# Token blocks of 512 and 256 in place of 384, with high and low parts side by side in one product

## The chip, the cores and the metric

One core of one Trainium2 chip runs the whole program. The metric is the device time of one execution in microseconds, the median of the runs shown. Engines: TensorE (PE; its weight loads are PEld), VectorE (DVE), ScalarE (ACT), GpSimd (POOL) and SyncE (SP), which issues most DMAs.

## What is computed

Four batches of 768 tokens, 8 heads of 48. A decaying state per head gives the attention's rows, which become x with 384 columns a token; a low-rank mix over the tokens and a two-layer channel mix follow:

```
for t in range(S):
    cur = einsum('bhd,bhe->bhde', u[None] * kt, vt)
    y[:, :, t] = einsum('bhd,bhde->bhe', rt, state + cur)
    state = w[None, :, :, None] * state + einsum('bhd,bhe->bhde', kt, vt)
...
u  = x + (x^T @ U @ V)^T              # U: 768 x 32, V: 32 x 768
out = u + max(u @ w_ch1, 0) @ w_ch2   # 384 -> 1536 -> 384, float32
```

## The kernel before, in words

The attention works in chunks of 128 tokens, six a batch. For batches 1 to 3, `a_chunk` (L1081) does a chunk's products in one go into the accumulator banks "mm" and "av", with the next chunk's scores and state in "tr" and "sc"; VectorE masks, keeps the state and adds the results into x (L1111).

After six chunks `c_g` (L1180) sums U^T x on TensorE (L1172) and splits it into G (L1192 to L1197). For batch 0 and the first block of batch 1 (`inside`), u is turned in TensorE: `c_x` transposes x into banks and `c_xu` adds the low-rank product there. For all other blocks `c_u` (L1199) corrects x by one product and one VectorE addition (L1205), `c_store` writes it to DRAM, `c_blocks` (L1270) reads it back in 32 x 32 blocks, and `c_turn` (L1273) transposes 384 tokens at a time on VectorE (L1279), copies the result to the high part uTh on ScalarE (L1281) and subtracts for the low part uTl on VectorE or GpSimd (L1282).

The channel mix takes a batch in two blocks of 384 tokens (TB, TPB = 3 chunks). The hidden layer has 12 slices of 128. For each slice f, `m_1` (L1290) makes 9 products of 384 columns into one of two "mm" banks: for each of three column tiles high W1 x high u, low W1 x high u, high W1 x low u. ScalarE rectifies into hh (L1305), VectorE makes the low part hl (L1306). `m_2` (L1312) makes 9 more products, three for each chunk, into three "acc" banks that run over all 12 slices; then VectorE adds the bank to x (L1348) and SyncE stores the rows (in the last block, ScalarE's queue). Every product loads its weights first; all these products go through the helper `whole` (L382), so they show as L385, and the names tell them apart: p<-uTh,w1s is `m_1`, p<-w2s,hh is `m_2`.

Every operation is handed to `Plan` with a key (a planned time) and a cost. `Plan.schedule` issues on each engine, in an order fixed at build time, the ready operation of lowest key. A batch's `mlp_units` are `m_1` of slice f + 1, then `m_2` of slice f, 49 units of PER = 1.85 a batch; the attention chunks of the next batch lie between them, from 6 after the batch's begin in steps of 10.0 (batches 2 and 3), with `c_g` at their end:

```
begin = [T0 + 49 * PER * b for b in range(B)]
t0, per = ((begin[b - 1] + 30, 8.0), (begin[b - 1] + 6, 10.0))[b > 1]
end = attention(b, t0, per, 5.0, 0)
at(end, lambda b=b: c_g(b))
```

Of the kernel before, what the change touches and what calls it, by code (L numbers as in the profile page):

```python
# [47 lines left out]
class Plan:  # L48
# [107 lines left out]
    def schedule(self):  # L156
# [12 lines left out]
        def admit(o):  # L169
# [8 lines left out]
            for b in o.allocs:  # L178
                ring = self.rings[b.tag]
                i = min((i for i, f in enumerate(ring["free"]) if f is not None), key=lambda i: ring["free"][i][0])  # L180
                o.ends.append(ring["free"][i])
                if ring["last"] is not None:
# [138 lines left out]
def rwkv_moe(ctx: ExitStack, tc: tile.TileContext, r, k, v, w, u, U, V, w1, w2, out):  # L321
# [14 lines left out]
    TB = 384  # L336
    NTB = S // TB
    TPB = TB // 128
    NX = 11
    NXS = 4  # L340
    NH = 4
    NR = 2
# [143 lines left out]
    pwi = cbuf([PD, NP, C], F32, "pwi")  # L486
# [209 lines left out]
    def a_load(n):  # L696
        b, c = divmod(n, NCH)
        if n < 4:
            t3 = xbuf([128, 2 * H * HP + DM], F32, "uTl" if n % 2 else "uTh", 2, f"ld_{n}")
# [16 lines left out]
        for i, src in ((1, k), (0, r), (2, v)) if n < NQA else ((0, r), (1, k), (2, v)):  # L716
            eng = "ACT" if n < NQA and i == 1 else "SP"
            dma(lambda q, i=i, src=src: q.dma_start(part(i)[:, :, :D], src[b, :, c * C:(c + 1) * C, :].rearrange("h p d -> p h d")),  # L718
                [ts[i] if n < 4 else (t3, i)] if n < 4 else [(ts[i], "d")], after_weights(n), 1024, 192, eng=eng, late=1300 if (n, i) == (0, 0) else 0)
# [460 lines left out]
    def c_g(b):  # L1180
# [9 lines left out]
        gf = wbuf([R, DM], F32, "xl", NXS, f"gf_{b}")  # L1190
# [22 lines left out]
    def c_x(b, t, i):  # L1213
# [3 lines left out]
        x = xs[b * NCH + t * TPB + i]  # L1217
# [5 lines left out]
    def u_bufs(b, t):  # L1223
        uT[b, t] = (xbuf([128, NCT, TB], F32R, "uTh", 2, f"uTh_{b}_{t}"),
                    xbuf([128, NCT, TB], F32R, "uTl", 2, f"uTl_{b}_{t}"))

    def c_xu(b, t):
        u_bufs(b, t)
        uh, ul = uT[b, t]
        for ct in range(NCT):  # L1230
            pt = upt[b, t][ct]
            pe(200, lambda ct=ct, pt=pt: whole(pt.t[:, :TB], lhsT=Gs[b].t[:, ct * 128:(ct + 1) * 128],
                                               rhs=V3.t[:, t * TB:(t + 1) * TB],
                                               start=False, stop=True, skip_group_check=True), [pt], [Gs[b], V3])
            on_act(384, lambda ct=ct, pt=pt: nc.scalar.copy(uh.t[:, ct, :], pt.t[:, :TB]), [(uh, ct)], [pt])
            on_dve(384, lambda e, ct=ct, pt=pt: e.tensor_tensor(ul.t[:, ct, :], pt.t[:, :TB], f32(uh.t[:, ct, :]),  # L1236
                                                                ALU.subtract), [(ul, ct)], [pt, (uh, ct)])

    def c_ut(b, i):
        n = b * NCH + i  # L1240
        t, j = divmod(i, TPB)
        if j == 0:
            u_bufs(b, t)
        uh, ul = uT[b, t]
# [3 lines left out]
        ptv = pt.t[:, :DM].rearrange("p (c t) -> p c t", c=NCT)  # L1248
        sl = slice(j * 128, (j + 1) * 128)
        nc.scalar.copy(uh.t[:, :, sl], ptv)  # L1250
        nc.vector.tensor_tensor(ul.t[:, :, sl], ptv, f32(uh.t[:, :, sl]), ALU.subtract)
# [14 lines left out]

    def c_blocks(b, t, ct):

        bt = ublk[b, t, ct] = wbuf([128, TPB, 128], F32, "xh", NXS, f"ub_{b}_{t}_{ct}")
        dma(lambda q: q.dma_start(bt.t, ud[b].t[t * TPB:(t + 1) * TPB, 4 * ct:4 * ct + 4].rearrange("j k t e -> (k t) j e")),  # L1270
            [bt], [(ud[b], (i, j)) for i in range(t * TPB, (t + 1) * TPB) for j in range(2)], 384, 512, late=1000)

    def c_turn(b, t, ct):  # L1273
        if ct == 0:
            u_bufs(b, t)
        uh, ul = uT[b, t]
        bt = ublk.pop((b, t, ct))
        ut = wbuf([128, TB], F32, "xl", NXS, f"ut_{b}_{t}_{ct}")
        on_dve(680, lambda e: e.transpose(ut.t.rearrange("p (j t m) -> p j m t", t=32, m=4),  # L1279
                                          bt.t.rearrange("p j (m c) -> p j m c", c=32)), [ut], [bt])  # L1280
        on_act(384, lambda: nc.scalar.copy(uh.t[:, ct, :], ut.t), [(uh, ct)], [ut])  # L1281
        on_either(384, lambda e: e.tensor_tensor(ul.t[:, ct, :], ut.t, f32(uh.t[:, ct, :]), ALU.subtract), [(ul, ct)],  # L1282
                  [ut, (uh, ct)])
# [4 lines left out]
    MM = 174  # L1288

    def m_1(b, t, f):  # L1290
        uh, ul = uT[b, t]
        pt = bank("mm", f"p1_{b}_{t}_{f}")

        def part(ct):
            wt = W1[f].t
            fs = slice(ct * 128, (ct + 1) * 128)
            o = pt.t[:, :TB]
            whole(o, lhsT=wt[:, 0, fs], rhs=uh.t[:, ct, :], start=(ct == 0), stop=False)
            whole(o, lhsT=wt[:, 1, fs], rhs=uh.t[:, ct, :], start=False, stop=False)
            whole(o, lhsT=wt[:, 0, fs], rhs=ul.t[:, ct, :], start=False, stop=(ct == NCT - 1))  # L1300
        for ct in range(NCT):
            pe(3 * MM, lambda ct=ct: part(ct), [pt], [(uh, ct), (ul, ct), W1[f]])
        hh = xbuf([128, TB], F32R, "hh", NH, f"hh_{b}_{t}_{f}")
        hl = xbuf([128, TB], F32R, "hl", NH, f"hl_{b}_{t}_{f}")
        on_act(384, lambda: nc.scalar.activation(hh.t, pt.t[:, :TB], AF.Relu), [hh], [pt])  # L1305
        on_dve(384, lambda e: e.scalar_tensor_tensor(hl.t, pt.t[:, :TB], 0.0, f32(hh.t), ALU.max, ALU.subtract),  # L1306
               [hl], [pt, hh])
# [4 lines left out]
    def m_2(b, t, f, first, last):  # L1312

        hh, hl = hs.pop((b, t, f))
        for i in range(TPB):
            n = b * NCH + t * TPB + i
            if first:
                ops[n] = bank("acc", f"p2_{n}_{f}")

        def high(i, pt):  # L1320
            ts_ = slice(i * 128, (i + 1) * 128)
            for half in range(2):
                whole(pt.t[:, :DM], lhsT=hh.t[:, ts_], rhs=W2[f].t[:, half], start=(first and not gates and half == 0), stop=False)

        def low(i, pt):
            ts_ = slice(i * 128, (i + 1) * 128)
            whole(pt.t[:, :DM], lhsT=hl.t[:, ts_], rhs=W2[f].t[:, 0], start=False, stop=last > 0)
        def gate(i, pt):
            whole(pt.t[:, :DM], lhsT=V3.t[:, (t * TPB + i) * 128:(t * TPB + i + 1) * 128], rhs=Gs[b].t, start=True, stop=False)
        gates = f == 0 and inside(b, t)  # L1330
        if gates:
            for i in range(TPB):
                pt = ops[b * NCH + t * TPB + i]
                pe(MM, lambda i=i, pt=pt: gate(i, pt), [pt], [Gs[b], V3])
        parts = [(part, m, h, i) for part, m, h in ((high, 2, hh), (low, 1, hl)) for i in range(TPB)]
        late = [0] * TPB
        if b == B - 1 and t == NTB - 1:

            late = [PER * x for x in {NFT - 3: (0, 2.3, 4), NFT - 2: (0, 0.4, 2.1), NFT - 1: (0, 0.1, 1.2)}.get(f, late)]
        for part, m, h, i in sorted(parts, key=lambda p: late[p[3]]):  # L1340
            n = b * NCH + t * TPB + i
            pe(m * MM, lambda part=part, i=i, pt=ops[n]: part(i, pt), [ops[n]], [h, W2[f]], dk=late[i])
        if last:
            for i in range(TPB):
                n = b * NCH + t * TPB + i
                x, pt = xs[n], ops[n]
                s0 = (t * TPB + i) * 128
                on_dve(384, lambda e, x=x, pt=pt: e.tensor_tensor(x.t, pt.t[:, :DM], x.t, ALU.add), [x], [pt])  # L1348
                left[n] = left.get(n, NFT) - last
# [9 lines left out]
    def mlp_runs(b):  # L1359
# [3 lines left out]
        cuts = [0, NFT // 3, 2 * NFT // 3, NFT]  # L1363
        runs, done = [], [0, 0]
        for i, c in enumerate(cuts[1:] + [NFT]):
# [4 lines left out]
    def mlp_units(b):  # L1370
# [3 lines left out]
        units = []  # L1374
        for i in range(len(steps) + 1):
            if i < len(steps):
                units.append(lambda s=steps[i]: m_1(b, s[0], s[1]))
            if i:
                units.append(lambda s=steps[i - 1]: m_2(b, *s))
# [246 lines left out]
```

## Time and profile before

| what | us |
|---|---|
| median of three runs | 401.51 (401.1 to 402.57) |
| the profiled execution | 402.06 |
| its span, first to last instruction | 400.3 |
| TensorE busy | 391.6 |
| VectorE busy | 270.6 |
| ScalarE busy | 132.4 |
| GpSimd busy | 88.0 |

The products of the channel mix run from about 42 us to 396 us with the attention's between them; batch 1's first product is near 138.8 us, batch 2's at 230.4, batch 3's at 321.0. A product's duration is its latency, and products overlap: what one costs is the distance from its start to the next one's. Windows give the busy time of each engine in a stretch; a wait names who waited and what ended it.

### The profile page before, as it was taken

What the parts mean: (1) busy time and instruction counts of PE and PEld (TensorE: products, weight loads), DVE (VectorE), ACT (ScalarE), POOL (GpSimd) and SP (SyncE); (2) the same over time, 40 slices, a digit from 0 to 9 for tenths busy, and PEclk for the clock granted to TensorE, in tenths of its full rate; (3) what the DMA queues carried; (4) which work ended last, traced back from release to release, by engine and by line L of the source; (5) the groups of instructions that cost most, each with busy time, mean ns of one, the idle gap of its engine ahead of it and who ended that gap; (6) DMA issues with size and microseconds to landing.
All of it is one profiled execution on the core that took longest, in us unless ns stands there. A gap on an engine that the chain in (4) does not pass through costs nothing.

```text
span 400.3 us, 11670 instructions
## 1 busy us (share of the span) xinstructions
PE 391.6 (98%) x4833; PEld 377.6 (94%) x4833; DVE 270.6 (68%) x626; ACT 132.4 (33%) x344; POOL 88.0 (22%) x136
## 2 busy tenths in 40 slices
PE   7999999999999999999999999999999999999995
PEld 7797899999999999999999999999999999999995
DVE  5797999999999778897684588876423661222112
ACT  3547968467851312110132240120113221111110
POOL 2972142244422114131140131231000120000000
PEclk9999999999999999999999999999999999999999
DMA  9989998799778685873797777510103630001001
GB/s 141 169 158 291 171 230 195 117 213 230 124 110 180 101 197 83 149 121 61 147 167 111 147 169 120 95 33 2 61 2 61 123 117 0 2 0 62 1 2 63
DMA packets 189993, 45.27 MB, mean 113 GB/s; under 512 B 174701, under 2 KB 188398, under 8 KB 189934
## 3 DMA queue, kind: packets, MB, share of 16 engines
q1 hardware_dynamic: 186382, 43.28, 55.4%
q10 hardware_dynamic: 3552, 1.18, 1.3%
q8 instruction: 40, 0.66, 0.7%
q14 instruction: 19, 0.16, 0.1%
HBM read 36.77 MB, written 7.67 MB: 111 GB/s over the span
## 4 chain that ended last, share of the span: by engine, by line
PE 92%; DVE 3%; SPq 1%; DMA 1%; ACT 1%; issue 0%; POOL 0%; POOLq 0%; DVEq 0%
PE p L385 75%; PE pav L901 3%; PE pav L907 3%; DMA ub<-in_u_dram 1%; PE pav L1053 1%; PE bank_tr L881 1%; SPq L718 1%; PE bank_tr L867 1%; PE bank_tr L1004 1%; PE bank_tr L1172 1%; PE pav L1059 1%; DVE uTl L1236 1%; PE bank_sc L867 1%; PE bank_tr L818 1%; DVE raw_w L612 1%; PE ptr L818 0%
## 5 line engine op out<-in xcount | busy, mean ns | idle before, releaser
L385 PE MATMUL p<-uTh,w1s 128*128 128x384 f32 x576 | 148.6, 338 | 0.2 <-DVE w1s L647 0.2
L385 PE MATMUL p<-w2s,hh 128*128 128x384 f32 x576 | 119.3, 337 | 0.2 <-ACT hh L1305 0.2
L1305 ACT ACTIVATE hh<-p 128x384 fp32r<-128x384 f32 x96 | 47.2, 492 | 216.5 <-PE p L385 216.4
L1306 DVE SCALAR_TENSOR_TENSOR hl<-p,hh 128x384 fp32r<-128x384 f32 x96 | 53.3, 555 | 89.6 <-ACT hh L1305 88.7
L385 PEld LDWEIGHTS p<-uTh,w1s 128*128 128x128 f32 x576 | 102.9, 188 | 1.3 <-DVE w1s L647 0.5
L385 PEld LDWEIGHTS p<-w2s,hh 128*128 128x128 f32 x576 | 100.6, 188 | 1.3 <-ACT hh L1305 0.5
L385 PE MATMUL p<-uTl,w1s 128*128 128x384 f32 x288 | 96.6, 335 | 0.0
L385 PE MATMUL p<-w2s,hl 128*128 128x384 f32 x288 | 66.6, 334 | 0.0
L385 PEld LDWEIGHTS p<-uTl,w1s 128*128 128x128 f32 x288 | 54.0, 188 | 0.3 <-DVE uTl L1236 0.3
L385 PEld LDWEIGHTS p<-w2s,hl 128*128 128x128 f32 x288 | 51.5, 188 | 0.0
L1282 POOL TENSOR_TENSOR uTl<-ut,uTh 128x384 fp32r<-128x384 f32 x7 | 7.1, 1016 | 71.3 <-ACT uTh L1281 71.3
L901 PEld LDWEIGHTS pav<-vsw,am 64*64 64x64 f32 x288 | 17.4, 134 | 4.5 <-issue 4.2
L901 PE MATMUL pav<-vsw,am 64*64 64x48 f32 x288 | 19.8, 221 | 0.0
L768 POOL MEMSET ks<- 128x128 f32 x24 | 4.7, 205 | 67.6 <-PE bank_tr L881 67.5
L901 PE MATMUL pav<-ldv,am 64*64 64x48 f32 x288 | 19.3, 221 | 0.0
L907 PE MATMUL pav<-S,rT 48*64 48x48 f32 x528 | 19.1, 218 | 0.0
L778 POOL TENSOR_TENSOR dv<-ldr,ldk 128x384 f32<-128x384 f32 x14 | 14.3, 1020 | 20.6 <-DVE wm L529 8.8
L907 PEld LDWEIGHTS pav<-S,rT 48*64 48x64 f32 x528 | 17.3, 135 | 0.0
L901 PEld LDWEIGHTS pav<-ldv,am 64*64 64x64 f32 x288 | 17.0, 134 | 0.0
L1348 DVE TENSOR_TENSOR x<-p,x 128x384 f32<-128x384 f32 x30 | 15.0, 549 | 2.8 <-PE p L385 2.3
L789 ACT ACTIVATE dv<-ldv,dg 128x48 f32<-128x48 f32 x56 | 13.4, 321 | 2.8 <-DVE dg L785 2.7
L1111 DVE TENSOR_TENSOR x<-pav,dv 128x192 f32<-128x192 f32 x36 | 11.9, 348 | 2.8 <-PE pav L907 2.8
(192 smaller groups left out, 565.5 us busy)
## 6 DMA issues: line engine op xcount, KB each, us to landing
raw_w<-in_moe_w_ch_dram SPq DMA_DIRECT2D x24, 384.0 KB, 4.6
out_dram<-x SPq DMA_DIRECT2D x21, 192.0 KB, 3.0
ldr<-in_r_dram SPq DMA_DIRECT2D x20, 192.0 KB, 3.7
ldk<-in_k_dram SPq DMA_DIRECT2D x20, 192.0 KB, 4.4
ldv<-in_v_dram SPq DMA_DIRECT2D x20, 192.0 KB, 4.4
bl<-in_r_dram SPq DMA_DIRECT2D x79, 48.0 KB, 2.4
bl<-in_k_dram SPq DMA_DIRECT2D x79, 48.0 KB, 2.7
ub<-ud SPq DMA_DIRECT2D x15, 192.0 KB, 3.3
```

The lines of the kernel that those rows point to most:

```text
L385: return nc.tensor.matmul(*args, **kw)
L768: op("POOL", 250, lambda: nc.gpsimd.memset(ks.t[:, :, D:], 0.0), [(ks, "pad")], [])
L778: on_either(384, lambda e, a_=a_, b_=b_: e.tensor_mul(dv.t, a_()[:, :, :D], b_()[:, :, :D]), w_, r_, only="POOL" if front(n) else None)
L789: nc.scalar.activation(dv.t[:, h], vt()[:, h], AF.Copy, scale=dg.t[:, h:h + 1])
L867: return [lambda q=q, i=i: nc.tensor.matmul(pt.t[(i ^ j) * C2:(i ^ j) * C2 + C2, q * C2:(q + 1) * C2], lhsT=kT.t[rows, q, i * C2:(i + 1) * ...
L901: return nc.tensor.matmul(to(q, j, i), lhsT=am[j].t[half, q, :], rhs=vsw[n].t[half, q, :] if j else vt()[half, 2 * q, :], start=((alone or ...
L907: return nc.tensor.matmul(to(q, row, i), lhsT=rT.t[rows, q, i * C2:(i + 1) * C2], rhs=St[n, i].t[rows, q, :], start=False, stop=((alone or ...
L1111: return e.tensor_tensor(heads(x.t), heads(avp[n][bank_].t[:, :DM]), heads(of), ALU.add)
L1282: on_either(384, lambda e: e.tensor_tensor(ul.t[:, ct, :], ut.t, f32(uh.t[:, ct, :]), ALU.subtract), [(ul, ct)], [ut, (uh, ct)])
L1305: on_act(384, lambda: nc.scalar.activation(hh.t, pt.t[:, :TB], AF.Relu), [hh], [pt])
L1306: on_dve(384, lambda e: e.scalar_tensor_tensor(hl.t, pt.t[:, :TB], 0.0, f32(hh.t), ALU.max, ALU.subtract), [hl], [pt, hh])
L1348: on_dve(384, lambda e, x=x, pt=pt: e.tensor_tensor(x.t, pt.t[:, :DM], x.t, ALU.add), [x], [pt])
```

## The change

Batches 1 to 3 take blocks of 512 and 256 tokens (4 and 2 chunks); batch 0 keeps 384. In the block of 512 the products of `m_1` have 512 columns, and `m_2` has a fourth chunk whose sums lie in the bank "av" and are added to x before each attention chunk that needs the bank (`cuts`). In the block of 256 the high and the low u lie side by side in one buffer: per column tile one product low W1 x high u (256 columns) and one high W1 x both (512 columns, the whole bank); VectorE adds the bank's halves into a new buffer `hs`, from which the rectifier and the low part read; `m_2` there is two units later, not one. Transposes are of 256 tokens. u's buffers become one ring of four, hl has three buffers for four, two rings of small buffers three for four, x has twelve for eleven; `c_u` takes two banks, not three. The keys change: units of 2.5 and 1.15 for the two blocks (1.85 in batch 0), attention chunks 9.3 apart, `c_g` and what follows 4.0 sooner.

```
-    TB = 384
-    NTB = S // TB
-    TPB = TB // 128
-    NX = 11
-    NXS = 4
+    NTB = 2
+    HB = 256
+    def tb(b, t):
+        return (512, 256)[t] if b else S // NTB
+    def joined(b, t):
+        return b > 0 and t == 1
+    NX = 12
+    NXS = 3
     NH = 4
+    NHL = 3
...
-        pt = bank(("tr", "sc", "av")[i % 3], f"ph_{n}") if b < B else bank("mm", f"ph_{n}")
+        pt = bank(("tr", "sc")[i % 2], f"ph_{n}") if b < B else bank("mm", f"ph_{n}")
...
+    class Parts:
+        def __init__(self, b, t):
+            self.n, self.joined = tb(b, t), joined(b, t)
+            self.bufs = [xbuf([128, NCT, 512 if b else self.n], F32R, "uT", 4, f"uT{'hl'[i]}_{b}_{t}") for i in range(2 - self.joined)]
+        def at(self, i, ct, lo=0, hi=None):
+            c0 = i * self.n if self.joined else 0
+            return self.bufs[0 if self.joined else i].t[:, ct, c0 + lo:c0 + (self.n if hi is None else hi)]
+        def both(self, ct):
+            return self.bufs[0].t[:, ct, :]
...
+        ut = wbuf([128, HB], F32, "xl", NXS, f"ut_{b}_{t}_{ct}_{g}")
+        on_dve(400, lambda e: e.transpose(ut.t.rearrange("p (j t m) -> p j m t", t=32, m=4),
+                                          bt.t[:, 2 * g:2 * g + 2].rearrange("p j (m c) -> p j m c", c=32)), [ut], [bt])
...
+            if joined(b, t):
+                whole(o, lhsT=wt[:, 1, fs], rhs=u.at(0, ct), start=(ct == 0), stop=False, skip_group_check=True)
+                whole(pt.t, lhsT=wt[:, 0, fs], rhs=u.both(ct), start=False, stop=(ct == NCT - 1), skip_group_check=True)
+                return
...
+        if joined(b, t):
+            rd = wbuf([128, HB], F32, "hs", 1, f"hs_{b}_{f}")
+            src = lambda: rd.t
+            on_dve(2 * n, lambda e: e.tensor_reduce(src(), pt.t.rearrange("p (i n) -> p n i", i=2), AX.X, ALU.add), [rd], [pt], dk=SUM)
...
+            if starts(b, t, f, i, first):
+                ops[n] = bank("acc" if i < 3 else "av", f"p2_{n}_{f}")
...
+            due.append(i)
+            while due and (i + 1 == len(steps) or due[0] + 1 + joined(b, steps[due[0]][0]) <= i):
+                j = due.pop(0)
+                units.append((steps[j][0], 2, steps[j][1], lambda s=steps[j]: m_2(b, *s)))
...
+    def starts(b, t, f, i, first):
+        return first if t or i < 3 or not 0 < b < B else cuts[b, f][0]
+    def ends_(b, t, f, i, last):
+        return last if t or i < 3 or not 0 < b < B else cuts[b, f][1]
+    def chunk_times(b):
+        t0, per = ((begin[b - 1] + 30, 8.0), (begin[b - 1] + 6, 9.3))[b > 1]
+        return t0, per
...
+        keys = [x for c in range(NCH) for t0, per in [chunk_times(b + 1)] for x in [t0 + per * c]] if b + 1 < B else []
...
+            end = f in ends or any(x < k <= ms[j + 1][0] for k in keys)
+            cuts[b, f] = (first, n if end else 0)
...
-    T0, PER = 44.0, 1.85
+    T0, PERS, SOON = 44.0, (2.5, 1.15, 1.85), 4.0
...
-            end = attention(b, t0, per, 5.0, 0)
+            end = attention(b, t0, per, 5.0, 0) - (SOON if b > 1 else 0)
```

## Rows read from the trace of the kernel before

**Rows 1.** The page: its first line, parts 1 and 4 (by engine).

```profile
span 400.3 us, 11670 instructions
...
PE 391.6 (98%) x4833; PEld 377.6 (94%) x4833; DVE 270.6 (68%) x626; ACT 132.4 (33%) x344; POOL 88.0 (22%) x136
...
PE 92%; DVE 3%; SPq 1%; DMA 1%; ACT 1%; issue 0%; POOL 0%; POOLq 0%; DVEq 0%
```

**Rows 2.** The chain of waits, 300 to 400 us: start us, us, what.

```profile
310.26 85.84 PE p L385 x495
396.09 0.02 issue
396.12 0.56 DVE x L1348
```

**Rows 3.** Windows by stage: us, busy us by engine (instructions), granted clock, DMA share, GB/s.

```profile
138.00:188.00 50.00, 49.77 (x790) 47.93 (x789) 40.83 (x101) 7.93 (x16) 12.79 (x20) 1.00 0.71 124
188.00:209.00 21.00, 21.00 (x280) 20.39 (x279) 15.63 (x37) 4.25 (x13) 5.78 (x6) 1.00 0.79 142
209.00:230.00 21.00, 21.00 (x163) 20.61 (x162) 11.18 (x20) 6.13 (x15) 1.02 (x1) 1.00 0.77 132
...
301.00:321.00 20.00, 20.00 (x123) 19.90 (x115) 10.19 (x19) 5.74 (x14) 1.01 (x1) 1.00 0.54 104
```

**Rows 4.** The list of waits: us in total, times, longest.

```profile
ACT hh L1305 <- PE p L385: 216.4, 82, 5.9
DVE hl L1306 <- ACT hh L1305: 88.7, 53, 2.8
```

**Rows 5.** Groups by line and shape, TensorE: count, busy us, mean ns, idle before.

```profile
L385 PE MATMUL p<-uTh,w1s 128*128 128x384 f32 x576 | 148.6, 338 | 0.2 <-DVE w1s L647 0.2
...
L385 PEld LDWEIGHTS p<-uTh,w1s 128*128 128x128 f32 x576 | 102.9, 188 | 1.3 <-DVE w1s L647 0.5
```

**Rows 6.** The timeline of PE from 39.2 us, other widths: start us, us.

```profile
39.01 0.60 PE L385 MATMUL pu<-ident,x 128*128 128x128 f32 x4
39.36 0.48 PE L385 MATMUL wake<-V 96*128 96x512 f32 x1
39.68 0.27 PE L385 MATMUL bank_tr<-ident,x 128*128 128x128 f32 x1
39.79 0.27 PE L385 MATMUL bank_sc<-ident,x 128*128 128x128 f32 x1
```

**Rows 7.** Groups by line and shape, VectorE and ScalarE.

```profile
L1306 DVE SCALAR_TENSOR_TENSOR hl<-p,hh 128x384 fp32r<-128x384 f32 x96 | 53.3, 555 | 89.6 <-ACT hh L1305 88.7
...
L1305 ACT ACTIVATE hh<-p 128x384 fp32r<-128x384 f32 x96 | 47.2, 492 | 216.5 <-PE p L385 216.4
...
L1348 DVE TENSOR_TENSOR x<-p,x 128x384 f32<-128x384 f32 x30 | 15.0, 549 | 2.8 <-PE p L385 2.3
...
L785 DVE TENSOR_REDUCE dg<-dv 128x8 f32<-128x384 f32 x24 | 12.9, 539 | 1.2 <-POOL dv L778 1.0
...
L1279 DVE STREAM_TRANSPOSE ut<-ub 128x384 f32<-128x384 f32 x15 | 12.3, 861 | 0.0
...
L835 DVE TENSOR_TENSOR rT<-ptr,pwi 112x512 f32<-112x512 f32 x5 | 3.4, 681 | 0.0
```

**Rows 8.** The chain of waits where batch 2's G is made.

```profile
209.45 1.13 PE bank_tr L1172 x48
```

**Rows 9.** SyncE's queue in the hand-over to batch 2: start us, us, count.

```profile
214.18 2.63 SPq L1261 DMA_DIRECT2D ud<-x  x3
...
221.22 2.76 SPq L1270 DMA_DIRECT2D ub<-ud  x3
```

**Rows 10.** The timeline of VectorE in the hand-over to batch 2.

```profile
225.40 2.44 DVE L1279 STREAM_TRANSPOSE ut<-ub 128x384 f32<-128x384 f32 x3
...
228.86 1.53 DVE L1282 TENSOR_TENSOR uTl<-ut,uTh 128x384 fp32r<-128x384 f32 x2 [0.25 <-ACT uTh L1281]
```

**Rows 11.** The timeline of PE: batch 2's first product.

```profile
230.44 0.51 PE L385 MATMUL p<-uTh,w1s 128*128 128x384 f32 x2
```

More of the change, by code (lines that the diff above doesn't have):

```diff
@@ new lines, in part @@
+            whole(o, lhsT=wt[:, 0, fs], rhs=u.at(0, ct), start=(ct == 0), stop=False)
+            whole(o, lhsT=wt[:, 1, fs], rhs=u.at(0, ct), start=False, stop=False)
+            whole(o, lhsT=wt[:, 0, fs], rhs=u.at(1, ct), start=False, stop=(ct == NCT - 1))
+        for ct in range(NCT):
+            rd = [(buf, (p, ct) + x) for p in range(2) for buf in [u.acc(p, ct)[0]]
+                  for x in ([()] if inside(b, t) else [(g,) for g in range(n // HB)])]
+            pe(347 if joined(b, t) else 3 * (14 + n / 2.4), lambda ct=ct: part(ct), [pt], rd + [W1[f]])
@@ L1314, in m_2 @@
         hh, hl = hs.pop((b, t, f))
[L1315 to L1318, printed above, removed]
+        for i in range(chunks(b, t)):
+            n = b * NCH + chunk_at(b, t) + i
+            if starts(b, t, f, i, first):
+                ops[n] = bank("acc" if i < 3 else "av", f"p2_{n}_{f}")
         def high(i, pt):
@@ L1322, in high @@
             for half in range(2):
-                whole(pt.t[:, :DM], lhsT=hh.t[:, ts_], rhs=W2[f].t[:, half], start=(first and not gates and half == 0), stop=False)
+                whole(pt.t[:, :DM], lhsT=hh.t[:, ts_], rhs=W2[f].t[:, half], start=(starts(b, t, f, i, first) and not gates and half == 0), stop=False)
         def low(i, pt):
             ts_ = slice(i * 128, (i + 1) * 128)
-            whole(pt.t[:, :DM], lhsT=hl.t[:, ts_], rhs=W2[f].t[:, 0], start=False, stop=last > 0)
+            whole(pt.t[:, :DM], lhsT=hl.t[:, ts_], rhs=W2[f].t[:, 0], start=False, stop=ends_(b, t, f, i, last) > 0)
@@ L1334, in m_2 @@
                 pe(MM, lambda i=i, pt=pt: gate(i, pt), [pt], [Gs[b], V3])
-        parts = [(part, m, h, i) for part, m, h in ((high, 2, hh), (low, 1, hl)) for i in range(TPB)]
-        late = [0] * TPB
+        parts = [(part, m, h, i) for part, m, h in ((high, 2, hh), (low, 1, hl)) for i in sorted(range(chunks(b, t)), key=lambda i: i < 3 or not ends_(b, t, f, i, last))]
+        late = [0] * chunks(b, t)
         if b == B - 1 and t == NTB - 1:
-            late = [PER * x for x in {NFT - 3: (0, 2.3, 4), NFT - 2: (0, 0.4, 2.1), NFT - 1: (0, 0.1, 1.2)}.get(f, late)]
+            late = [PERS[1] * x for x in {NFT - 2: (0, 1.3), NFT - 1: (0, 0.4)}.get(f, late)]
@@ L1402, in slow_path @@
             d = nc.sync.dma_start(wb[i * H:(i + 1) * H], w)
-            for o in stored[-TPB:] if i == 0 else ():
+            for o in stored[-chunks(B - 1, 1):] if i == 0 else ():
                 tc.add_manual_dep(d.ins, o.ins.name,
@@ L1541, in rwkv_moe @@
     end = attention(0, FRONT, EACH, 2.0, 0)
-    for i in range(3):
+    for i in range(chunks(0, 0)):
         at(end + 0.1 + 0.1 * i, lambda i=i: c_x(0, 0, i))
@@ L1548, in rwkv_moe @@
         if b:
[L1549 removed]
+            t0, per = chunk_times(b)
             for c in range(NCH):
@@ L1567, in rwkv_moe @@
             if inside(b, 0):
-                for i in range(3):
+                for i in range(chunks(b, 0)):
                     at(end + 0.1 + 0.1 * i, lambda b=b, i=i: c_x(b, 0, i))
@@ L1571, in rwkv_moe @@
             else:
-                for i in range(TPB):
+                for i in range(chunks(b, 0)):
                     at(end + 0.2 + 0.1 * i, lambda b=b, i=i: (c_u(b, i), c_store(b, i)))
```

196 lines of the change are left out of this document (109 added, 87 removed).

## The prediction

> **What bounds the kernel now.** I read the page first, then the chain of waits, the windows and the list of waits. TensorE is busy for 391.6 of 400.3 us and holds 92% of the chain that ended last [rows 1], so time is lost or won on TensorE, or where something new makes it wait. The late chain shows how dense it is: 495 products of the channel mix end to end in 85.84 us, broken only at 396.09 us [rows 2], then one VectorE addition and the last store. In batches 1 and 2 the windows give TensorE 49.77 of 50.00, 21.00 of 21.00 and 21.00 of 21.00 us [rows 3]; the granted clock is 1.00, the level of 2.4 GHz. There is no wait to remove, so the change can win only by cheaper products. The other engines wait for TensorE: ScalarE's rectifier 216.4 us, VectorE's low part of h 88.7 us for that rectifier [rows 4]. That is the cover under which new VectorE work would lie. It is uneven: VectorE is busy 40.83 of 50.00 us while batch 2's attention runs, 15.63 of 21.00 after, 11.18 of 21.00 in the hand-over, 10.19 of 20.00 in the last one [rows 3].
>
> **The products.** 85.84 us / 495 = 173.4 ns from one 384-column product to the next [rows 2]; at 2.4 GHz 384 columns are 160.0, so 13.4 ns are left over. The 338 ns of the page's group is the latency of one, overlapped with the next [rows 5]. For each slice f of the hidden layer a batch has now 2 blocks x (9 + 9) = 36 products of 384 columns, 13,824 columns. After the change the first block has 9 products of 512 and 12 of 384, the second 3 of 256, 3 of 512 and 6 of 384: 33 products, and 4608 + 4608 + 768 + 1536 + 2304 = 13,824 columns. So the columns stay; 3 products fewer x 12 slices x 3 batches = 108 go, with whatever a product costs beyond its columns. The second product of W2, 384 columns each, is untouched, as is batch 0.
>
> Neither 512 nor 256 columns against freshly loaded weights stands in a long row, so I bound them. 256: not under the spacing of whole-array 128-column products, each with its own load, which begin 0.11 us apart [rows 6], nor over the 173 of the 384-column ones. 512: not under 213.3, its columns at the granted clock. From above there is one row: the transposes from 39.01 us are 0.11 apart, so the fourth begins near 39.34, and the next transpose after the 512-column product begins at 39.68; 0.34 less one transpose's 0.11 is 0.23 to 0.24, taken as 0.237 [rows 6]. For one slice the first layer then costs, from below, 9 x 213.3 + 3 x (110 + 213.3) = 2890 ns, from above 9 x 237 + 3 x (173 + 237) = 3363, against 18 x 173.4 = 3121 now. Over 36 slices that is -8.3 to +8.7 us. Between such ends I take the nearest row, the 384-column one with the same operand types: columns at 2.4 GHz plus the same 13.4 ns. 512 is then 226.7, 256 is 120.1, a slice 9 x 226.7 + 3 x (120.1 + 226.7) = 3081, and the gain 40 ns x 36 = **1.45 us** (108 x 13.4).
>
> That the rest is per product is an assumption. If it went with the columns, 13.4/160 = 8.4% of each, 512 would take 231 and 256 115.6: equal columns, equal time, gain nothing. The single 512-column row, 0.23 to 0.24, lies nearer to this. The Trainium skill, page "TensorE: Matmul & The Clock Gate", section "Back-to-back issue gap", gives a warm product as N/2.4 plus 2.5 ns; by it 384 columns would be 162.5, where the row has 173.4, and the 108 products would return 0.27 us. Here the measurement decides for more than 2.5; which part of it is per product no row settles.
>
> **Small TensorE edits.** Batch 1's first block is turned inside TensorE: four chunks, not three, so 3 more transposes at 0.11 [rows 6], +0.33; its three closing products grow by 128 columns, 3 x 53 ns, +0.16; one product that starts an accumulator is added and one that added h to x is dropped, 0. Together **+0.49 us**. The stores and turned blocks of batches 2 and 3 use no TensorE.
>
> **What VectorE gets.** For each joined slice one sum of 512 accumulator columns into 256. No row has that access. From below, 0.54 us, the reduction of 384 elements; from above, 512 elements at the price of the costliest pattern, 861/384 = 2.24 ns each, 1.15 us; I take 0.68, VectorE's pass over 512 columns of an accumulator, whose reading it resembles most [rows 7]. The low part of h costs 0.555 at 384 [rows 7]; at 512 and 256, by 1 ns a column, 0.69 and 0.42: the sum over the batch is unchanged. The nine transposes of 256 cost, at 2.24 ns, 0.57 each, 5.2 us against 6 x 0.861 = 5.2: nothing. In batches 1 and 2 the fourth chunk's sums lie in the bank that attention uses, so they are added to x before each attention chunk: up to 6 more additions of 0.55. So a batch has 12 x 0.68 = 8.2 us more, batches 1 and 2 up to 11.5. Of batch 1's 92 us (138 to 230) VectorE is busy 40.83 + 15.63 + 11.18 = 67.6 [rows 3], 74%; it becomes 79.1, 86%. GpSimd can take some of it. I cost this at 0 because it lies beside TensorE, but half of the free time is used up.
>
> **The chain through a joined slice.** Products, sum 0.68, rectifier on 256 columns about 0.42 (0.492 at 384, 0.6 ns a column) and low part 0.42 make 1.52 us; with 0.35 for the drain and the semaphores 1.9, or 2.35 with the dearest sum. Behind it the order puts two more first-layer units and two second-layer units before the slice's own second product: 4 x 1.04 = 4.2 us. The bank of the first layer is free after the sum, about 1.0 to 1.5 us, and needed after 3.1. Queued behind the sum on VectorE are the low part and, in batches 1 and 2, the attention's and next block's steps. Cost 0; with VectorE late by 2.1 us the cover is gone, and TensorE waits for each further one. At the very end two second-layer units, 2.1 us, lie between the last first-layer product and its second product, which needs 1.5: still covered. What follows the last product [rows 2] is the same addition and store.
>
> **The hand-over to batches 2 and 3.** Before a batch starts, its attention sum G is made on TensorE, x is corrected, stored, read back in blocks, transposed and split. In batch 2 G's products begin at 209.45 us [rows 8], the stores at 214.18, the reads at 221.22 [rows 9], the transposes at 225.40, the last low part ends at 230.39 [rows 10], and the first product starts at 230.44 [rows 11]: 21.0 us of work in 21.0 us of cover, nothing to spare for later slices. With 512 tokens one more chunk goes through: a correction and its bank +0.7, a store +1.4 (the wait of the third of those stores on SyncE's queue, within the 2.63 of the three), a third more bytes in the reads +1.1, transposes 6 x 0.57 against 2.44, +1.0: about 25.2. The change moves G earlier: its key is 6 + 6 x 9.3 - 4.0 = 57.8 after the batch's, and with 2.5 a unit the 23 units before 57.5 and the second block's first one go ahead of it. One second-layer unit of 2.1, 23 x 1.04 and 6 corrections of 0.17 remain, 27.0 us. So 1.8 are spare by this sum, if attention is ready; the attention steps, VectorE's included, are pulled into 9.3 in place of 10.0 planned us a chunk. I put **+0.3 us** for new waits: two hand-overs and twelve shared-bank turns, with half of one addition's 0.55 exposed.
>
> **The sum.** The profiled execution took 402.06 us, its span 400.3 and 1.8 around it. 402.06 - 1.45 + 0.49 + 0.3 = 401.4. It lies 0.55 over the median of the three runs, 401.51; on the median's scale the forecast is 400.8 us.
>
> **Rivals.**
> (a) The rest goes with the columns: no gain, +0.49 and +0.3, 402.3 on the median's scale. For it: the one 512-column row. Against it: that row stands beside transposes, whose neighbours also differ from 173.
> (b) A product of 256 columns waits for its weight load. A load's record is 188 ns whatever the product [rows 5]; if 256 columns don't cover it, they cost 173.4 like 384. Then 36 x 3 x 53.3 = 5.8 us come on top: 406.6, slower. It decides where the spacing passes 133 ns (the gain of 13.4 lost). Against it: whole-array loads with 128 columns pass at 0.11 us [rows 6]. The Trainium skill, page "TensorE: Matmul & The Clock Gate", section "LDWEIGHTS (loading the stationary operand)", prices 128 columns of weights at 107 ns, about what 256 columns take at 2.4 GHz; by it the load would just be hidden, and the trace's 0.11 us agrees.
> (c) The hand-over, the one on the other side that I take most seriously: VectorE at 86% brings the last attention chunk late, G starts later than 25.2 us before the batch's last product, and TensorE idles by the excess, twice. With G 4 us later than ordered, 2.2 us each, 4.4: 405.2, slower. For it: rows 10 and 11 show no slack now. Against it: 5 to 6 us more cover, and GpSimd's room, busy 12.79 of 50.00 and 5.78 of 21.00 [rows 3].
> (d) A long stream hides the rest altogether: 512 at 213.3, 256 at 120: 9 x 213.3 + 3 x 333.4 = 2920, 201 x 36 = 7.2 us won, 395.0. Against it: the 512-column row.
>
> **Chances.** Forecast 0.58, by itself 399.2 to 401.8; (a) 0.13; (b) 0.07; (c) 0.17; (d) 0.05. About 0.5%, 2.0 us, is what can be told from no change: bounds 399.5 and 403.5. Of the forecast 0.14 lies under 399.5, where waits are fewer and the rest larger; with (d) 0.19 faster. (b) and 0.14 of (c), where the excess is large, make 0.21 slower; 0.60 is the same. The range leaves out (d), the upper half of (b) and (c): 398.9 to 404.8.
>
> **What would show it.** Right: TensorE's long run at 3081 + 3121 ns a slice in batch 3, with 227 and 120 as spacings; no idle at the hand-overs; first-layer unit 2.04 us and 1.04 us. Wrong: a 512 spacing of 231 (a), a 256 spacing near 173 (b), TensorE waiting at a batch's first product for the turned u (c), or for the sum, or at the shared bank. A sum far over 0.68 us would make VectorE the bound in the second blocks.

## The result

405.43 us median of 5 (404.83 to 406.0), the kernel before 401.52 of 5 (401.1 to 402.95): 1.0088 times as long, 95% interval 1.0065 to 1.0112. That is 3.9 us slower, outside the range of 398.9 to 404.8. The profiled execution took 405.82 us.

### The profile page after: what moved, and what is told of

Read it like the earlier page. It is cut to its first block, busy times and chain, and to the rows that moved or that the text cites. A ratio compares the mean times of both kernels' runs of the same rounds, so it can differ in the third digit from the quotient of the medians.

```text
span 404.0 us, 11587 instructions
## 1 busy us (share of the span) xinstructions
PE 393.4 (97%) x4728; PEld 359.6 (89%) x4728; DVE 297.5 (74%) x677; ACT 140.2 (35%) x370; POOL 91.6 (23%) x140
## 4 chain that ended last, share of the span: by engine, by line
PE 90%; DVE 4%; SPq 2%; DMA 2%; issue 1%; ACT 0%; DVEq 0%
PE p L397 74%; PE pav L913 3%; PE pav L919 3%; DMA ld<-in_r_dram 2%; SPq L730 1%; PE bank_tr L893 1%; PE pav L1065 1%; PE bank_tr L879 1%; PE bank_tr L1016 1%; PE bank_tr L1184 1%; PE pav L1071 1%; DVE uTl L1261 1%; PE bank_sc L879 1%; PE bank_tr L830 1%; PE bank_tr L397 1%
## 5 line engine op out<-in xcount | busy, mean ns | idle before, releaser
L397 PE MATMUL p<-uTh,w1s 128*128 128x256 f32 (+2 forms) x576 | 149.2, 360 | 0.2 <-DVE w1s L659 0.2
L1351 ACT ACTIVATE hh<-p 128x512 fp32r<-128x512 f32 (+1 forms) x60 | 33.3, 555 | 144.3 <-PE p L397 144.2
L1352 DVE SCALAR_TENSOR_TENSOR hl<-p,hh 128x512 fp32r<-128x512 f32 (+1 forms) x60 | 38.1, 635 | 54.2 <-ACT hh L1351 53.3
L397 PE MATMUL p<-uTl,w1s 128*128 128x512 f32 (+1 forms) x180 | 67.1, 373 | 0.0
L397 PEld LDWEIGHTS p<-uTl,w1s 128*128 128x128 f32 x180 | 33.8, 188 | 4.7 <-DVE uTl L1261 0.3
L1351 ACT ACTIVATE hh<-hs 128x256 fp32r<-128x256 f32 x36 | 15.1, 418 | 61.6 <-DVE hs L1350 61.2
L1350 DVE TENSOR_REDUCE hs<-p 128x256 f32<-128x512 f32 x36 | 24.7, 686 | 9.5 <-PE p L397 8.1
L1395 DVE TENSOR_TENSOR x<-p,x 128x384 f32<-128x384 f32 x42 | 21.7, 550 | 5.4 <-PE p L397 4.9
L1352 DVE SCALAR_TENSOR_TENSOR hl<-hs,hh 128x256 fp32r<-128x256 f32 x36 | 15.6, 434 | 12.0 <-ACT hh L1351 11.9
L1315 POOL TENSOR_TENSOR uTl<-ut,uTh 128x256 fp32r<-128x256 f32 x7 | 5.1, 738 | 65.6 <-ACT uTh L1314 63.4
```

Source lines behind the costliest of these rows:

```text
L397: return nc.tensor.matmul(*args, **kw)
L1315: on_either(HB, lambda e: e.tensor_tensor(u.at(1, ct, *sl), ut.t, f32(u.at(0, ct, *sl)), ALU.subtract), [key(1)], [ut, key(0)])
L1350: on_dve(2 * n, lambda e: e.tensor_reduce(src(), pt.t.rearrange("p (i n) -> p n i", i=2), AX.X, ALU.add), [rd], [pt], dk=SUM)
L1351: on_act(n, lambda: nc.scalar.activation(hh.t[:, :n], src(), AF.Relu), [hh], [rd], dk=SUM if joined(b, t) else 0.0)
L1352: on_dve(n, lambda e: e.scalar_tensor_tensor(hl.t[:, :n], src(), 0.0, f32(hh.t[:, :n]), ALU.max, ALU.subtract), [hl], [rd, hh], dk=SUM if ...
```

## The profile after

First the page: its first line and lines of parts 1 and 4 (answers to [rows 1]).

```profile
span 404.0 us, 11587 instructions
...
PE 393.4 (97%) x4728; PEld 359.6 (89%) x4728; DVE 297.5 (74%) x677; ACT 140.2 (35%) x370; POOL 91.6 (23%) x140
...
PE 90%; DVE 4%; SPq 2%; DMA 2%; issue 1%; ACT 0%; DVEq 0%
```

There are 105 TensorE products fewer, and yet 1.8 us more of TensorE; "issue" has come up from 0% to 1%. The windows by stage (us, busy us by engine (instructions), clock, DMA share, GB/s; answers to [rows 3], the later one 1 us earlier):

```profile
138.00:188.00 50.00, 49.23 (x830) 43.32 (x832) 40.89 (x97) 10.01 (x25) 12.88 (x19) 1.00 0.70 120
...
208.00:229.00 21.00, 20.73 (x118) 19.18 (x117) 17.57 (x35) 5.62 (x14) 1.75 (x3) 1.00 0.75 142
```

VectorE (third number) has 17.57 of 21.00 us in the hand-over, for 11.18 before, and TensorE still idles only 0.27 there. 49.23 in the first window is less than the 49.77 before: something stops TensorE inside batch 1. VectorE's groups (answers to [rows 7]):

```profile
L1352 DVE SCALAR_TENSOR_TENSOR hl<-p,hh 128x512 fp32r<-128x512 f32 x36 | 24.9, 691 | 53.6 <-ACT hh L1351 53.1
L1350 DVE TENSOR_REDUCE hs<-p 128x256 f32<-128x512 f32 x36 | 24.7, 686 | 9.5 <-PE p L397 8.1 <-DVE hl L1352 0.5
...
L1352 DVE SCALAR_TENSOR_TENSOR hl<-hs,hh 128x256 fp32r<-128x256 f32 x36 | 15.6, 434 | 12.0 <-ACT hh L1351 11.9
```

The hand-over to batch 2 and batch 2's first product, on PE's timeline (answers to [rows 8, 11]):

```profile
209.28 0.42 PE L397 MATMUL bank_tr<-Gs,V 96*128 96x384 f32 x1 [0.27 <-DVE Gs L1207]
...
230.89 0.63 PE L397 MATMUL p<-uTh,w1s 128*128 128x512 f32 x2
```

0.27 us for G, nothing at the first product of 512. So not the hand-over. The timeline of batch 3 gives the cost of the units (a unit is one layer's products of one slice in one block) from start to start (answers to [rows 2]); first a unit of 512 and its second layer, then a joined unit and its second layer:

```profile
329.38 0.39 PE L397 MATMUL p<-uTh,w1s 128*128 128x512 f32 x1
...
331.46 1.57 PE L397 MATMUL p<-w2s,hh 128*128 128x384 f32 x8
...
333.57 0.63 PE L397 MATMUL p<-uTh,w1s 128*128 128x512 f32 x2
...
381.78 1.21 PE L397 MATMUL p<-uTh,w1s 128*128 128x256 f32 x6
382.82 0.87 PE L397 MATMUL p<-w2s,hh 128*128 128x384 f32 x4
...
383.89 0.28 PE L397 MATMUL p<-uTh,w1s 128*128 128x256 f32 x1
```

9 products of 512: 331.46 - 329.38 = 2.08 us (forecast 2.04). 12 of 384: 333.57 - 331.46 = 2.11 (12 x 173.4 are 2.08). The joined unit: 1.04, as forecast. 6 of 384: 1.07 (1.04). The mean starts of all such units in batch 3 make a slice 2081 + 2106 + 1043 + 1069 = 6299 ns, where the kernel before takes 4 x 1560 = 6240 and the forecast said 3081 + 3121 = 6202. The products of the second layer, which the change doesn't touch, have become dearer. The kernel before goes from layer to layer as often, with 384 columns in both, and each of its units takes 1.56 us:

```profile
339.75 1.20 PE L385 MATMUL p<-w2s,hh 128*128 128x384 f32 x6
...
341.31 0.51 PE L385 MATMUL p<-uTh,w1s 128*128 128x384 f32 x2
...
342.88 0.85 PE L385 MATMUL p<-w2s,hh 128*128 128x384 f32 x4
```

So it is not the change of operands or of banks that costs, but something that came with the widths.

The second loss stands in the chain of waits (start us, us, what; the two longest stops):

```profile
168.80 0.77 issue
...
251.38 0.92 issue
```

and in PE's list of waits (us in total, times, longest):

```profile
PE bank_tr L893 <- issue: 1.7, 2, 0.9
...
PE bank_tr L397 <- DVE Gs L1207: 0.3, 1, 0.3
```

Twice TensorE stops inside an attention chunk, between two small products, and nothing that the profile shows ends the wait. The starts are 0.98 and 1.13 us apart, where 0.01 to 0.05 is usual there.

**Where the time went.** From the first product of the channel mix to the end of the last, the two profiles of before that there are in the end take 353.97 us (42.11 to 396.08) and 353.94 (41.73 to 395.67), the one of after 358.21 (40.69 to 398.90): +4.24. Each product is counted by the distance from its start to the next one. The channel mix's products go from 300.10 to 301.38, **+1.28** (forecast -1.45); of those, a start that came over 30 ns late, at attention or a pause, is counted at the forecast's price for its width. Attention's products, in which the two stops lie, go from 41.14 to 43.32, **+2.18**; transposes of x, closing products and products with G from 5.49 to 6.25, +0.77 (forecast 0.49). That leaves 0.01. What lies ahead of the stretch and behind it differs from execution to execution by about as much as between the kernels: 42.11 + 4.27 and 41.73 + 5.87 us before, 40.69 + 5.12 after.

## The experiments

All ratios are to the kernel before on the same chip.

**1. Without the joined product.**

```
-        return b > 0 and t == 1
+        return False
```

> The blocks of 512 and 256 tokens stay; only the joined product goes: the second block makes 9 products of 256 columns a slice, VectorE sums nothing, and the second product follows one unit later, not two. Theory A (a product costs its columns, 13/12 of the time at 2.4 GHz, nothing by itself): the 108 products that come back cost nothing, 256-column starts lie 115.6 to 116.5 ns apart, batch 3's first layer in the second block stays at 1.04 us a slice, VectorE is 24.7 us less busy (about 273 us), and the time is that of the changed kernel, 405.4 us, ratio 1.009, less what its two stalls inside attention gave if they go away. Theory B (13.4 ns for each product beside its columns, the forecast): +1.45 us, 406.9, ratio 1.012, 256-column starts 120 ns apart. Theory C (VectorE's sum or the longer chain is what lengthens the changed kernel): 2 us or more come back, 403.4 or less, ratio 1.005 or less.

406.21 us, ratio 1.0114 (1.0090 to 1.0138). PE's timeline, one slice of the second block in batch 3:

```profile
379.86 0.40 PE L397 MATMUL p<-uTh,w1s 128*128 128x256 f32 x2
...
380.93 0.86 PE L397 MATMUL p<-w2s,hh 128*128 128x384 f32 x4
...
381.98 0.40 PE L397 MATMUL p<-uTh,w1s 128*128 128x256 f32 x2
```

9 products of 256 take 1.07 us, then 6 of 384 take 1.05: 2.12 a slice where the joined kernel has 2.11 (1.04 and 1.07). What joining saves in the first layer, the second layer gives back. Over three batches, counted as above, the 108 products cost 0.24 us (301.62 for 301.38), not 1.45. VectorE, 21 us lighter, brings nothing: theory C falls. A and B both miss, since 256 took 118.5 ns, between their numbers. The time says less than the products: this run has one of the two stops, and in its shorter order TensorE waits 0.8 us for VectorE's low part of h at 318.66, which the changed kernel doesn't.

**2. Trains of one width, and widths mixed.**

```
+    for n in (512, 480, 384, 320, 288, 256, 192, 128):
+        products(f"r{n}", [512] + [n] * 36, xr, wr)
+    products("mixA", ([512] * 9 + [384] * 12) * 4, xr, wr)
+    products("mixB", ([256, 512] * 3 + [384] * 6) * 6, xr, wr)
+    products("same", [512] + [384] * 108, xr, wr)
```

> Computes none of the reference: only trains of TensorE products, each with its own 128-column weight load, operands of the kernel's type, one width at a time (512, 480, 384, 320, 288, 256, 192, 128), then widths mixed as in the changed kernel's blocks (512 with 384; 256, 512 and 384), and the same widths in bf16. Start to start at a granted clock of 1.00. Theory A (the rest goes with the columns): 231, 216.7, 173.3, 144.4, 130, 115.6 ns, that is 13/12 of columns / 2.4, mixes add nothing, and one product of 512 costs two of 256. Theory B (13.4 ns for each product): 226.7, 213.4, 173.4, 146.7, 133.4, 120.1. Theory C (widths mixed disturb the 384-column ones): in the mixes the 384-column starts lie 1 to 3 ns further apart than in the train of 384 alone. Below some width the weight load sets the spacing: at 128 columns 110 ns or less is expected, as between whole-array transposes.

PE's timeline, one window inside each train, and the trains of mixes from start to start:

```profile
23.67 6.96 PE L35 MATMUL p_r<-xr,wr 128*128 128x512 f32 x30
39.38 5.54 PE L35 MATMUL p_r<-xr,wr 128*128 128x384 f32 x31
56.30 3.64 PE L35 MATMUL p_r<-xr,wr 128*128 128x256 f32 x29
64.32 3.96 PE L35 MATMUL p_r<-xr,wr 128*128 128x128 f32 x34
...
68.23 16.94 PE L35 MATMUL p_mixA<-xr,wr 128*128 128x512 f32 x84
85.00 12.84 PE L35 MATMUL p_mixB<-xr,wr 128*128 128x256 f32 x72
97.68 19.12 PE L35 MATMUL p_same<-xr,wr 128*128 128x512 f32 x109
```

A row lasts from the first start to the last end; less the last product's latency (0.39, 0.33, 0.28, 0.27), over one product fewer, it gives 226.6, 173.7, 120.0 and 112 ns; the 384s settle at 173.3. So in a run of one width the forecast's price holds at 512, 384 and 256, 13.3 ns over the columns: theory B there, and rival (a) falls as a mechanism. It is no fixed fee at every width, though: 320 columns have 13.3 too, but 480 alternate between 213 and 221 ns to the end of their run, 16.7 over on average, and 288 lie 11.7 over. Theory C holds as well: at the prices of the runs mixA is 36 x 226.6 + 48 x 173.4 = 16.48 us, and it takes 85.00 - 68.23 = 16.77. The starts show how: the first six products of 384 after a 512 lie 171, 175, 178, 185, 176 and 182 ns apart, 27 over six settled ones, and only then 173, 173, 174; nine of 512 behind 384s take 41 ns more than settled ones. That is the pattern of the changed kernel: its 6 products of 384 behind a joined unit are 175, 175, 177, 185, 176, 182, so none is ever settled.

**3. More breaks, and fewer, by themselves.**

```
+    products("pairB", ([256, 512] * 6 + [384] * 12) * 3, xr, wr)
+    products("one", [384] * 24 + ([128] + [384] * 12) * 4, xr, wr)
+    products("apart", ([256] * 9 + [384] * 6) * 6, xr, wr)
+    products("joined", [256, 512] * 30, xr, wr)
+    products("turns", [512, 384] * 24, xr, wr)
+    products("bA", ([512] * 9 + [384] * 12) * 4, xb, wb)
+    products("bB", ([256, 512] * 3 + [384] * 6) * 6, xb, wb)
```

> Computes none of the reference: trains of TensorE products with their weight loads, as before, now in runs twice as long (18 of 512 with 24 of 384; 6 times 256 and 512 with 12 of 384), with one product of 128 columns in every 13th place, with 9 of 256 and 6 of 384, with 256 and 512 in turn throughout, with 512 and 384 in turn throughout, and two of the mixes in bf16. Theory A (each break in the cadence costs a settling): the 384s behind 24 others cost 173.4 after their sixth; the one short product brings back 27 ns in the next six; 256 and 512 in turn hold 348 to 350 ns a pair, 3 to 5 over 13.4 a product; 512 and 384 in turn never settle and cost 405 or more a pair where settled runs give 400; in bf16, whose products lay 2.2 to 2.5 ns over their columns in long runs, the mixes cost the same as the runs. Theory B (each width has its own price): 227 to 231, 173.4 to 175 and 116 to 120 in every order, 401 a pair for 512 and 384 in turn.

PE's timeline, train by train:

```profile
38.63 12.72 PE L35 MATMUL p_pairB<-xr,wr 128*128 128x256 f32 x72
51.19 13.12 PE L35 MATMUL p_one<-xr,wr 128*128 128x384 f32 x76
64.15 12.84 PE L35 MATMUL p_apart<-xr,wr 128*128 128x256 f32 x90
76.83 10.57 PE L35 MATMUL p_joined<-xr,wr 128*128 128x256 f32 x60
87.24 9.92 PE L35 MATMUL p_turns<-xr,wr 128*128 128x512 f32 x48
97.00 15.75 PE L35 MATMUL p_bA<-xb,wb 128*128 128x512 bf16 x82
```

The row to compare is p_apart: 76.83 - 64.15 = 12.68 us for 90 products, and p_mixB of experiment 2, the same columns in 72 products, 97.68 - 85.00 = 12.68. Joined or not, the same. p_pairB, with half the changes of width, takes 12.56. 512 and 384 in turn take (97.00 - 87.24) / 24 = 407 ns a pair, for 400 in settled runs (theory A); 256 and 512 in turn 347 (a pair of settled ones 346.7), so the change of width within a joined unit costs nothing that shows, against theory A's 348 to 350. One product of 128 columns brought back 172 and 179 before 173, not six slow ones: a miss in the size. In p_apart the 384s behind nine of 256 lie 177, 174, 175, 174, 173 and 173 ns apart, 7 over settled ones in all, and the 256s behind 384 even come below theirs. So what a change costs depends on the two widths, and why is open. In bf16 a start lies 1.7 to 3.3 ns over its columns, in mixes as in runs (three records are missing there): of the two operand types tried, only the one that this kernel uses shows the settling. The Trainium skill, page "TensorE: Matmul & The Clock Gate", section "Back-to-back issue gap", has N/2.4 plus 2.5 ns as the gap of a single warm product; the bf16 trains show it back to back, each product with its own load (216 and 162.5 ns at 512 and 384).

**4. The same products, units in pairs.**

```
+            order = [(1, 0)] + [x for i in range(1, n - 3, 2) for x in ((1, i), (1, i + 1), (2, i - 1), (2, i))]
```

> The changed kernel with the units of the channel mix of batches 1 to 3 in pairs: two first-layer units, then two second-layer units, in place of one and one; the same products, half as many changes from one width to another. Theory A (after each change of width TensorE needs about six to nine products until its cadence has settled, which costs some 41 ns when 9 products of 512 begin and 26 to 28 ns when those of 384 begin): 18 products of 512 take 4121 ns, not 2 x 2081, 24 of 384 take 4187, not 2 x 2106, and in the second block 12 of 384 take 2109, not 2 x 1069. That is 95 ns a pair of slices, 18 pairs, of which the ends of the batches and the attention between them spare some: 1.0 to 1.7 us less in the products, time 404.0, ratio 1.005 to 1.0065. Theory B (512 columns cost 231 and 384 cost 175 here whatever stands before them): no change in the products, 405.4, ratio 1.009. The stalls inside attention may move with the order, so the products' starts decide, and the time only beside them.

403.42 us, ratio 1.0048 (1.0029 to 1.0067), at the lower edge of theory A's range. PE's timeline in batch 3, two second-layer units in a row:

```profile
327.00 1.57 PE L397 MATMUL p<-w2s,hh 128*128 128x384 f32 x8
...
329.11 1.55 PE L397 MATMUL p<-w2s,hh 128*128 128x384 f32 x8
...
331.19 0.63 PE L397 MATMUL p<-uTh,w1s 128*128 128x512 f32 x2
```

The first 12 products take 2.11 us, the second 12, the very same kind of work, 2.08. 18 of 512 took 4121 ns, 24 of 384 took 4186. The products of the channel mix, counted as above, came down by 1.0 us to 300.4, which is theory A's. The stretch went further, from 358.21 to 355.39: one of the two stops had gone and the other was shorter (0.61 us from start to start, for 0.98), which nobody had asked of this edit. So the forecast of the time came out in part by luck.

**5. TensorE's instructions some 100 further on.**

```
+            for _ in range(2):
+                whole(bank_.t[:32, :1], lhsT=still[:, :32], rhs=still_[:, :1], start=False, stop=True, skip_group_check=True)
```

> The changed kernel with two products of one column added to each filler that keeps TensorE awake at the start; they write the filler's bank, which nothing reads. Every later instruction of TensorE keeps its place in the order, but stands some 100 instructions further down the stream. Theory A (the two stalls of about 1 us inside attention products, at 168.6 and 251.2 us in the changed kernel, come from the supply of TensorE's instructions, which is a matter of the position in the stream): the stalls leave those two products (the scores' and state's transposes of the same chunks are then gap-free) and either vanish, 403.3 us, ratio 1.004, or stand at other places about 100 instructions earlier in the work. Theory B (a wait on VectorE, a bank or a semaphore that the profile doesn't name): both stalls stay at the same two products with the same length, 405.5, ratio 1.009.

413.94 us, ratio 1.0313 (1.0290 to 1.0336): the fillers make the start 9 us longer (first product at 49.75), against both expectations of the time. The stretch behind is 356.41 us for 358.21, and PE's list of waits, whole:

```profile
PE wake L397 <- DVE still L425: 1.0, 1, 1.0
PE pu L397 <- DVE Gs L1209: 0.5, 1, 0.5
PE bank_tr L397 <- DVE Gs L1209: 0.3, 1, 0.3
PE p L397 <- DVE w1s L661: 0.2, 1, 0.2
```

Both stops are gone from their places, with the order of the work unchanged, which theory B forbids. A shorter one has come up in the attention chunk before: at 167.88 us a start lies 0.34 us behind the last one, with only 0.13 us of it idle, which the list doesn't have. In each of the seven stops listed in attention (after, and experiments 1, 4, 6 and 7), a 16 KB packet of the queue called "instruction" begins 1.2 to 1.9 us ahead of the last start before the stop, and 173 to 256 of TensorE's instructions (195 and 204 in the changed kernel) have run since. That fits theory A, but it doesn't show it. In the changed kernel itself 243 instructions run in the 1.7 us behind the packet of 82.15 us, and TensorE goes on; in experiment 8 it is the same at 157.24. And experiment 7, whose edit touches no instruction of TensorE, has only one of the two stops. So the position in the stream alone doesn't decide, a stop that is missing from one profile need not have been removed by the edit, and the cause of the stops stays open.

**6 and 7. The last store.** The last two stores of after are issued on ScalarE's queue, the first in 0.37 us, the second, 1.04 us behind, in 1.25; the kernel before has 0.34 for its last.

```
-                        ... eng="ACT" if b == B - 1 and t == NTB - 1 else "SP")
+   6:                   ... eng="ACT" if b == B - 1 and t == NTB - 1 and i == 0 else "SP")
+   7:                   ... eng="ACT" if b == B - 1 and t == NTB - 1 and i else "SP")
```

> The changed kernel with the very last store of the output issued on SyncE's queue; the other store of the last block stays on ScalarE's. Theory A (the last store is late because it is issued on ScalarE's queue close behind the other one: 1.25 us for the issue where the kernel before has 0.34): the end after the last product shrinks from 5.1 to about 4.2 us, the time by 0.9 to 404.5 us, ratio 1.0065. Theory B (a store near the end takes 1.25 or 1.3 us to issue on any queue, or the DMA itself is later): no change, 405.4, ratio 1.009.

> The changed kernel with the first of the last block's two stores on SyncE's queue and the very last one on ScalarE's, the other way round than in the run with the last store on SyncE, where the store was issued in 0.33 us but SyncE's jump past the second program began only then and took 2.7 us. Theory A (two stores 1.04 us apart on one queue hold each other up; a queue that issues nothing last has its jump behind it): the last store is issued in 0.3 to 0.4 us instead of 1.25, the end after the last product is 4.2 us instead of 5.1, time 404.5, ratio 1.0065. Theory B (the jump of whichever engine comes last sets the end, and ScalarE's is as long): no change, 405.4, ratio 1.009.

407.09 us, 1.0141 (1.0117 to 1.0165), and 405.39 us, 1.0099 (1.0069 to 1.0128). The timeline of the queues at the end, first of run 6, then of run 7:

```profile
399.51 0.37 ACTq L1400 DMA_DIRECT2D out_dram<-x  x1
...
400.57 0.33 SPq L1400 DMA_DIRECT2D out_dram<-x  x1
```

```profile
397.21 0.33 SPq L1400 DMA_DIRECT2D out_dram<-x  x1
...
398.26 0.37 ACTq L1400 DMA_DIRECT2D out_dram<-x  x1
```

Apart, both are issued quickly, as theory A said, but the end is no sooner: 6.2 and 5.4 us behind the last product. In both, SyncE jumps past the second program (the kernel's slow path, which isn't run) only at the end and goes on 2.7 and 3.0 us later; VectorE's jump took 3.1 us in both, and 3.0 in after. Experiment 7 is theory B's time; experiment 6 came out slower than either theory allows. The last store doesn't explain the 3.9 us either: the second profile of before, with its last store issued in 0.34, ended 5.87 us behind its last product.

**8. Pairs, and 48 instructions more.**

```
+            if len(awake) == 7:
+                for g in range(12):
+                    nc.tensor.matmul(bank_.t[g % 4 * 32:g % 4 * 32 + 32, :1], lhsT=still[:, :32], rhs=still_[:, :1], ...)
```

> The run with the units in pairs, and 12 products of 32 rows and one column (48 instructions of TensorE) in one filler at the start, where TensorE then waits for a load; they write the filler's bank, which nothing reads. Theory A (instruction supply): the one stall left there, at 168.5 us, is gone, 0.5 us, and the time is 403.0 us, ratio 1.0037, if the 12 products cost nothing where they lie. Theory B: it stays, 403.4 to 404.0, ratio 1.005 to 1.006. By either theory the products of the channel mix are those of the pairs run within 0.1 us: 307.1 us, the same as in the kernel before, and what is left against that one is the extra transposes and closing products of batch 1 (0.75) and the end (0.7).

402.98 us, ratio 1.0049 (1.0028 to 1.0071). The stop is gone and the stretch 354.81 us (355.39 with pairs alone), the products where they were. In the ratio to the kernel before the 0.5 us does not show; the first product came 0.8 us later (41.52 for 40.73). Against the kernel before, pairs are still slower; the changed kernel's own ratio is 1.0088.

**9 and 10. The kernel before, shifted, and as it is.**

> The kernel before, with the same edit that took both stalls out of the changed kernel: two one-column products more in each filler at the start, some 100 instructions of TensorE ahead of all the rest; the start gets about 8 us longer by them, as it did there, so the time itself says nothing. Theory A (a stall inside attention comes when a packet of TensorE's instructions is fetched just as some 200 of them run off in 1.3 us): shifted by 100 instructions, two fetches of the kernel before fall on the starts of two dense attention stretches, at 157 and 260 us of its own trace, and stalls of 0.5 to 1.1 us appear 1.3 us behind them, at about 167 and 270 us here, where the kernel before has none. Theory B (the stalls belong to the changed kernel's own waits): none appear.

> The kernel before as it is, for a second profile. Theory A (the 1.4 us by which the changed kernel's first product came sooner are the spread of the start, since its programme there is the same but for buffers): the first product of the channel mix lies anywhere between 40.5 and 42.1 us. Theory B (the start really gained): it lies at 42.0 to 42.2 again. By both, no stall inside attention, all 384-column units of batch 3 at 1560 ns, and the last store's issue under 0.4 us with the one ahead of it at 1.3.

Shifted as in experiment 5 it took 408.97 us (one run), its stretch 353.93, with no stop, against theory A. The packets of the instruction queue did not come where the count of instructions said, but 2 to 3 us later, at the ends of the dense stretches (167.1 and 268.7 us). So no stop was made to order, and the forecast of where the packets fall was wrong. As it is: 403.25 us (one run), first product at 41.73, last at 395.67. The kernel before has such a stop too, ahead of the channel mix, in its first and second profile:

```profile
PE pav L1053 <- issue: 0.7, 1, 0.7
```

```profile
PE pav L1053 <- issue: 1.0, 1, 1.0
```

The changed kernel's own profile has none there, which may be part of its earlier first product.

## Why the prediction was wrong

- **The step that failed** is "108 x 13.4" in the part on the products. The 13.4 ns were read rightly, and 512 and 256 have them too in long runs of their own (experiment 2). What failed is that 512, 256 and 384 were priced as if each stood in such a run, as the 384s of [rows 2] do. In place of the 40 ns a slice to be saved, going between the widths costs 41 + 26 + 3 + 28 = 98 ns over these prices in batch 3. In batches 1 and 2 attention breaks the cadence in both kernels, so in the whole stretch it is less than 36 times that: -1.45 became +1.28. Undoing the joining cost 0.24, and halving the changes gave 1.0 back, so this part of the loss is shown by experiment; why TensorE needs the settling is not.
- Rival (a) came nearest in number for the products (231 and 116 ns in the mean starts), but by another mechanism; experiment 2 tells them apart. Its one witness, the 0.237 of [rows 6], was a product standing between other widths. The 405.2 of rival (c) lies closest to the measured 405.43, by accident: its waits at the hand-overs did not come.
- **The step that was missing:** two stops of TensorE, 2.2 us, in attention's products, which the change doesn't touch. Nothing in the rows ahead of the prediction named them; the kernel before has one only ahead of the channel mix. In the one profile of after they are the largest part of the loss, and their cause stays open. By these sums either miss alone, 2.7 us in the products (-1.45 forecast, +1.28 measured) or 2.2 in the stops, would have left the time inside the range; together they put it outside.
- The small TensorE edits cost 0.77, not 0.49: the transposes 0.40 for 0.33, the wider closing products 0.17 for 0.16, and 0.20 for the products with G that correct x, which the forecast left unchanged.
- VectorE: the sum 0.686 us for 0.68, the low part 0.691 and 0.434 for 0.69 and 0.42. It took 27 us more, and TensorE's waits show no cost of it, as said; the cover held (experiment 1).
- The hand-over: 0.27 us of wait at G and none at the first product, for "+0.3": right, and rival (c) with it wrong. Rival (b): 256 columns take 120 in a run of their own, and below that the spacing stops falling with the columns (112 at 192 and at 128): wrong. Rival (d): 512 at 226.6, not 213: wrong.

## What to carry to other kernels

A spacing read from a long run of equal products prices that run, not the same product between others: before splitting or widening products, look in the trace, or in a short train of the same order, for what the first products after each change of width cost. It isn't every change: 384 behind 512 cost 27 ns, 512 and 256 in turn nothing. Joining two products saves their fixed part only where the cadence stays settled; the same work in pairs gave back more than the joining saved. A wait that ends in "issue" inside dense small products came and went with edits elsewhere, so compare kernels over the stretch that they share, and over more than one profile, before explaining a difference of a microsecond or two.

## What the runs showed of the hardware

- With this operand type the first six products of 384 columns behind 512 took 27 ns more than settled ones, nine of 512 behind 384 took 41 more, six of 384 behind nine of 256 took 7 more (experiments 2 and 3); bf16 products show none of it, and lie 2 to 3 ns over their columns in place of 13.3.
- Spacings of a long run with this operand type: 226.7 ns at 512 columns, 173.3 at 384, 120.0 at 256, and 112 both at 192 and at 128.
- Stops of 0.6 to 1.3 us from start to start in dense small products, listed in five runs of the changed kernel and its variants, each had a 16 KB packet of the instruction queue 1.2 to 1.9 us ahead; other such packets had no stop behind them.
- A store issued 0.7 to 1.05 us behind another on one queue took 1.0 to 1.36 us to issue (after, experiments 1, 4, 5 and 8), alone 0.33 to 0.37; an engine's jump over the second program took up to 3.1 us at the end.
